# Feed-forward tiles finished in the attention slots: tanh and two products from PSUM, and one stored tile instead of two

## The chip, the cores and the metric

The kernel runs on one core of a Trainium2 chip. The metric is the device time of one execution in microseconds, as the median of several runs; smaller is better. TensorE (PE in the profile, PEld its weight loads) multiplies, VectorE (DVE), ScalarE (ACT) and GpSimd (POOL) work on elements, and SyncE (SP) issues most DMAs. Each engine takes its instructions in the order in which the program lists them, and engines wait for each other by semaphores.

## The reference

The layer mixes sliding-window attention and a gated feed-forward block by a sigmoid gate per row. S = 2048 rows, D = 512, 32 heads of 16, a window of 256, F = 1792.

```python
def _A_ref(x, wqkv, wo):                       # attention
    qkv = (x @ wqkv).reshape(B, S, 3, H, Dh) ...
    scores = einsum("bhqd,bhkd->bhqk", q, k) * (Dh ** -0.5)
    mask = (idx[:, None] - idx[None, :] >= 0) & (idx[:, None] - idx[None, :] < W)
    p = softmax(where(mask, scores, -1e9))
    return einsum("bhqk,bhkd->bhqd", p, v) ... @ wo
def _B_ref(x, w_gate, w_up, w_down):           # feed-forward
    return (silu(x @ w_gate) * (x @ w_up)) @ w_down
g = sigmoid((x * gate_w).sum(-1, keepdims=True))
return g * a + (1 - g) * b
```

## The kernel before

Every float32 product is made of three matmuls of a rounded high part and a low part (`xhi`, `xlo`, `wh`, `wl`), accumulated in PSUM. The work has three stages.

1. A start (about 80 us): x is split, q and k of the first two of eight head groups (four heads each) and all of v are computed, and the first scores of group 0.
2. The attention slots: 8 groups x 16 blocks = 128 slots t, with g = t // 16. A slot has four head steps. In each, `stage1` makes a score product of the next group for the row maximum (PE L275, tile `ps1`; DVE L277 masks it and takes the maximum, and so frees the PSUM bank), `stage2` makes a transposed score product of the present group (PE L314, tile `ps2`), whose exp ScalarE writes to `pt` (ACT L316) and GpSimd masks (L318, L321), and a "turn" adds six matmuls of 64 rows (PE L225), two at a time on the two halves of the array. In group 7 there is no `stage1` left, and `stage2` makes its score products two at a time. Every fourth slot (t % 4 = 0), after head step 1, `av` makes the weighted sum of 512 query rows (PE L338), which `finish` normalises in five steps over the following slots (L353 to L368).
3. The tail: the feed-forward's second product for all tiles and the output projection, 963 matmuls of 128 x 512.

The turns are projections that fill TensorE in the slots. A unit is one key: `("f", f, 0)` is the gate projection of feed-forward tile f (128 hidden columns by 2048 rows), `("f", f, 1)` its up projection, `("p", g)` the q and k of group g. `lanes` computes two 512-row chunks at once: in its first turn the first chunk gets the upper half of the contraction and the second chunk the lower half, in its second turn it is the other way round. The two turns write the same two banks from different halves of the array, so the second must not begin before the first is over. `lanes` sees to it by a dependence of the second turn's first matmuls on an instruction that follows the first turn:

```python
if second and i == 0:
    tc.add_manual_dep(mm.ins, BEHIND[mark[0]].ins.name, SYNC, reason="the first turn is over")
if i == n - 1:
    mark.append(len(BEHIND))
```

`BEHIND` is a list to which `stage2` appends each exp as it is written down (`stage1` appends its maxima in group 0 alone, ahead of the slots). `mark` holds the place of the next entry after the first turn's last matmul.

A unit takes four slots, with two pairs of chunks in banks `pa` and `pb` (each name has two banks): the order is `[a0, b0, a1, b1]`, one turn per slot. When a pair is done, ScalarE copies both banks to tiles `ev` (L522, `kept()`, five of them) and SP stores the copies in the DRAM array `raws` (L525). `AT` holds, for a slot and head step, the functions that `later` puts there; they run after that step's turn. The tail loads gate and up again (L689), ScalarE takes the silu (L703), VectorE multiplies (L704), and `split` makes the high and the low part for the second product. The tile of f = 13 alone is computed in the tail (L700). `prepare` splits the next unit's weights (ScalarE L67, GpSimd L70) and fetches the weights after those.

The order on each engine is the order in which this code is written out; no scheduler moves anything.

Of the kernel before, what the change touches and what calls it, by code (L numbers as in the profile page):

```python
# [9 lines left out]
F32 = mybir.dt.float32  # L10
# [23 lines left out]
def gated_mix(ctx, tc, xT, xn, wqk, wv, wo, wgu, wd, gw, out):  # L34
# [114 lines left out]

    WKEYS = list(UNITS)  # L150
    WKEYS += [("f", NF - 1, i) for i in range(2)]
# [22 lines left out]
    with ExitStack() as A:  # L174
# [151 lines left out]
        def av(g, c):  # L326


            AV[g, c] = (pp.tile([P, CH], F32, name="pb" if 4 * g + c + 1 < len(UNITS) else "pa"),
                        ps1.tile([P, CH], F32, name="ps1") if 4 * g + c + 1 >= 4 * (G - 1) else ps2.tile([P, CH], F32, name="ps2"))  # L330

            orders = [[4 * c + m for m in ms if 4 * c + m >= 0] for ms in ((0, 1, 2, -1, -2, 3), (0, 1, -1, 2, 3, -2))]
            for n, kbs in enumerate(zip(*orders)):
                for j in range(4):
                    for h, (o, kb) in enumerate(zip(HALVES, kbs)):
                        k0 = kb * P + 64 * h
                        q0, q1 = max(k0, c * CH), min(k0 + W + 64, c * CH + CH)
                        nc.tensor.matmul(AV[g, c][h][32 * j:32 * j + 32, q0 - c * CH:q1 - c * CH],  # L338
                                         VG[4 * g + kb // 4][o, kb % 4, 17 * j:17 * j + 32],
                                         PT[g, kb, j // 2][o, j % 2, q0 - kb * P:q1 - kb * P],  # L340
                                         start=n == 0, stop=n == len(orders[0]) - 1, skip_group_check=True)
# [170 lines left out]
        def unit(key, t):  # L512


            later(t, 3, prepare)

            def done(hf):
                def copies(ps):
                    t0 = t + 3 + hf
                    places = [kept(), kept()]  # L520
                    for m in range(2):
                        later(t0, 2 * m if t0 < G * NB else 0, lambda m=m: nc.scalar.copy(places[m], ps[m]))  # L522
                    if key[0] == "f":
                        for m in range(2):
                            later(t0 + 1, 2, lambda m=m: nc.sync.dma_start(raws[key[1], key[2], 2 * hf + m], places[m]))  # L525
                        return
                    g = key[1]

                    def half(m):
                        if m == 0:  # L530
                            X[g, hf] = x_pair()
                        split_qk(g, hf, m, places[m])
                    t1 = t0 + 3 * hf
                    later(t1, 3, lambda: half(0))
                    later(t1 + 1, 1, lambda: half(1))
                    later(t1 + 1, 3, lambda: stack(g, hf))
                return copies
# [43 lines left out]
        def tile0_load():  # L581
            for i, place in enumerate(halves_of(halves_of(KT[1][1])[0])):
                GOT[ORDER[0], i, 0] = place.bitcast(F32)
                nc.sync.dma_start(GOT[ORDER[0], i, 0], raws[ORDER[0], i, 0])

        def tile0():
            (gt, up), sg = [GOT.pop((ORDER[0], i, 0)) for i in range(2)], kept()
            nc.scalar.activation(sg, gt, AF.Silu)
            nc.vector.tensor_tensor(out=sg, in0=up, in1=sg, op=ALU.mult)
            split(*TILE0, sg, nc.scalar, nc.vector)  # L590
# [7 lines left out]
        for t in range(G * NB + 1):  # L598
            g, i = divmod(t, NB)
            d, part = divmod(t, NSLOT)  # L600
            if part == 0:
                turns = unit(UNITS[d], t) if d < len(UNITS) else [iter(())] * NSLOT
            s1 = stage1(g + 1, i) if t < g7 else iter(())
            s2 = stage2(g, i) if t < G * NB else iter(())
            for hd in range(4):
# [5 lines left out]
                run(turns[part], 3)  # L611
# [20 lines left out]
    with ExitStack() as B:  # L632
        hp = B.enter_context(tc.tile_pool(name="hp", bufs=3, side="right"))
        got = B.enter_context(tc.tile_pool(name="got", bufs=4, side="right"))
# [50 lines left out]
        def load_kept(c, f):  # L685

            for i in range(2):
                GOT[f, i, c] = got.tile([P, CH], F32, name=f"got{i}")
                nc.sync.dma_start(GOT[f, i, c], raws[f, i, c])  # L689

        def hidden(c, f):
            gu = []
            for i, name in enumerate(("pa", "pb")):
                if (f, i, c) in KEPT:
                    gu.append(GOT.pop((f, i, c)))
                    continue
# [6 lines left out]
            nc.scalar.activation(sg, gu[0], AF.Silu)  # L703
            nc.vector.tensor_tensor(out=sg, in0=gu[1], in1=sg, op=ALU.mult)  # L704
# [46 lines left out]
        for _ in range(3):  # L751
            load_kept(*loads.pop(0))
# [64 lines left out]
```

## Time and profile before

| | |
|---|---|
| median of 3 runs | 822.22 us (821.8 to 822.39) |
| span of the profiled execution, first to last instruction | 821.5 us |
| slots / tail in it | about 79.5 to 599 / 599 to 821.5 us |
| busy share of PE, DVE, ACT, POOL | 99%, 63%, 55%, 43% |
| granted TensorE clock | 1.000 |
| instructions | 21573 |

The page of the profile gives no other time of the profiled execution than its span. Rows of a timeline have the start and the length in us, engine, source line, operation, output tile <- input tiles, shape, and in brackets the idle time ahead of it and what ended it. A group's row has count, busy us and mean ns of one, and idle time ahead with its releasers. Matmul lengths are modelled, and neighbours overlap; what counts is the distance of their starts.

### The profile page before, as it was taken

How to read it: one execution, taken by the hardware profiler on the slowest of the kernel's cores; microseconds unless marked ns; L12 is line 12 of the kernel's file. 1: busy time of each engine (PE TensorE's matmuls, PEld its weight loads, DVE VectorE, ACT ScalarE, POOL GpSimd, SP SyncE). 2: the span in 40 equal slices, each digit the busy share in tenths (PEclk: the TensorE clock that was granted, in tenths of full speed). 3: DMA queues.
4: the chain of work that ended last, by engine and by line, in shares of the span. 5: the costliest groups of instructions: out<-in, count | busy, mean ns of one | idle time of the engine just before them, and what ended most of it. 6: DMA issues, size and time to landing. Idle time of an engine off the chain costs nothing.

```text
span 821.5 us, 21573 instructions
## 1 busy us (share of the span) xinstructions
PE 815.1 (99%) x8329; PEld 683.8 (83%) x8329; DVE 515.6 (63%) x1437; ACT 448.9 (55%) x936; POOL 351.8 (43%) x640
## 2 busy tenths in 40 slices
PE   8999999999999999999999999999999999999998
PEld 7888988888888888888888888888887888888886
DVE  6397677677667676677677667756567453443543
ACT  6422666666656666666666666656654433333341
POOL 7812555555546555645554655456511221011020
PEclk9999999999999999999999999999999999999999
DMA  8574534624534543552562463466698563383531
GB/s 294 164 206 150 154 121 125 191 94 146 166 128 125 161 146 117 152 170 101 144 193 102 126 191 125 160 207 201 210 325 267 182 197 110 131 244 107 178 125 51
DMA packets 67957, 133.26 MB, mean 162 GB/s; under 512 B 11600, under 2 KB 16336, under 8 KB 67856
## 3 DMA queue, kind: packets, MB, share of 16 engines
q1 hardware_dynamic: 63888, 118.00, 46.3%
q0 software_dynamic: 3968, 13.90, 4.6%
q8 instruction: 65, 1.06, 0.6%
q14 instruction: 36, 0.29, 0.1%
HBM read 61.08 MB, written 45.61 MB: 130 GB/s over the span
## 4 chain that ended last, share of the span: by engine, by line
PE 95%; DMA 2%; DVE 1%; ACT 1%; issue 1%; SPq 0%; DVEq 0%; ACTq 0%
PE pb L225 24%; PE pa L225 24%; PE pb L338 7%; PE ps L275 6%; PE ps L87 5%; PE ps L85 5%; PE ps L86 5%; PE ps L314 5%; PE pb L205 2%; PE pa L205 2%; PE pb L85 2%; PE pb L87 2%; PE pb L86 2%; PE ps L338 2%; DMA got<-raws 1%; PE pb L700 1%
## 5 line engine op out<-in xcount | busy, mean ns | idle before, releaser
L277 DVE CUSTOM_DVE_ANT_0 ps<-ps,mask 128x384 f32<-128x384 f32 (+2 forms) x512 | 271.6, 539 | 143.2 <-PE ps L314 66.7
L316 ACT ACTIVATE pt<-ps 128x384 f32<-128x384 f32 (+2 forms) x512 | 240.7, 477 | 114.9 <-PE ps L275 57.7
L318 POOL TENSOR_SCALAR_AFFINE_SELECT pt<-pt 128x256 f32<-128x256 f32 x256 | 107.4, 419 | 223.8 <-ACT pt L316 220.4
L314 PE MATMUL ps<-q,k 64*128 64x384 f32 (+2 forms) x512 | 159.9, 329 | 0.0
L275 PE MATMUL ps<-k,q 63*128 63x384 f32 (+2 forms) x512 | 158.7, 330 | 0.0
L225 PE MATMUL pb<-xhi,wh 64*128 64x512 f32 x512 | 111.3, 394 | 0.0
L225 PE MATMUL pb<-xlo,wh 64*128 64x512 f32 x512 | 110.1, 391 | 0.0
L225 PE MATMUL pb<-xhi,wl 64*128 64x512 f32 x512 | 109.9, 392 | 0.0
L225 PE MATMUL pa<-xhi,wh 64*128 64x512 f32 x512 | 109.0, 394 | 0.0
L225 PE MATMUL pa<-xhi,wl 64*128 64x512 f32 x512 | 107.9, 391 | 0.0
L225 PE MATMUL pa<-xlo,wh 64*128 64x512 f32 x512 | 107.8, 391 | 0.0
L275 PEld LDWEIGHTS ps<-k,q 63*128 63x128 f32 x512 | 88.8, 185 | 16.9 <-issue 5.7
L321 POOL TENSOR_SCALAR_AFFINE_SELECT pt<-pt 128x256 f32<-128x256 f32 x224 | 98.7, 441 | 0.0
L314 PEld LDWEIGHTS ps<-q,k 64*128 64x128 f32 x512 | 89.9, 184 | 5.4 <-issue 0.8
L704 DVE TENSOR_TENSOR sg<-got,sg 128x512 f32<-128x512 f32 x51 | 45.1, 885 | 64.6 <-ACT sg L703 59.9
L338 PE MATMUL ps<-pt,vg 64*32 64x320 f32 (+4 forms) x1408 | 75.0, 346 | 0.0
L338 PE MATMUL pb<-pt,vg 64*32 64x320 f32 (+3 forms) x1360 | 73.9, 350 | 0.0
L277 DVE DVE_READ_ACCUMULATOR2_ANT mx<- 128x1 f32 x512 | 71.9, 140 | 0.0
L338 PEld LDWEIGHTS pb<-pt,vg 64*32 64x32 f32 x1360 | 46.4, 106 | 28.3 <-ACT pt L316 9.9
L225 PEld LDWEIGHTS pb<-xhi,wh 64*128 64x128 f32 x512 | 56.6, 185 | 7.9 <-ACT ev L522 0.3
L225 PEld LDWEIGHTS pb<-xhi,wl 64*128 64x128 f32 x512 | 56.5, 184 | 6.7
L225 PEld LDWEIGHTS pa<-xhi,wl 64*128 64x128 f32 x512 | 54.7, 184 | 7.4
(159 smaller groups left out, 1576.6 us busy)
## 6 DMA issues: line engine op xcount, KB each, us to landing
raws<-ev SPq DMA_DIRECT2D x104, 256.0 KB
got<-raws SPq DMA_DIRECT2D x102, 256.0 KB
od<-o POOLq DMA_DIRECT2D x32, 256.0 KB, 2.6
raw<-wgu SPq DMA_DIRECT2D x28, 256.0 KB
q<-xhi SPq DMA_DIRECT2D x56, 128.0 KB
k<-xhi SPq DMA_DIRECT2D x56, 128.0 KB
vd<-vs POOLq DMA_DIRECT2D x8, 672.0 KB, 5.1
vg<-vd SPq DMA_DIRECT2D x32, 168.0 KB
```

Of the source, the lines that this page charges most:

```text
L85: nc.tensor.matmul(ps, lh, rh, start=start and i == 0, stop=False, skip_group_check=skip)
L86: nc.tensor.matmul(ps, lh, rl, start=False, stop=False, skip_group_check=skip)
L87: nc.tensor.matmul(ps, ll, rh, start=False, stop=stop and i == n - 1, skip_group_check=skip)
L225: mm = nc.tensor.matmul(ps[me], w[r], x[r], start=not second and i == 0, stop=bool(second) and i == n - 1)
L275: nc.tensor.matmul(ps[:, :n], QT[g % 2][pr][r, q0:q0 + P], KT[g % 2][pr][r, k0:k0 + n], start=True, stop=True)
L277: mx = nc.vector.tensor_tensor_reduce(out=ps[:, :n], in0=ps[:, :n], in1=mask[:, 3 * P - n:], scale=1.0, scalar=NEG, op0=ALU.add, op1=ALU.m ...
L314: nc.tensor.matmul(ps[:, :n], KT[g % 2][pr][r, k0:k0 + P], QT[g % 2][pr][r, k0:k0 + n], start=True, stop=True)
L316: BEHIND.append(nc.scalar.activation(pt[:, j, :n], ps[:, :n], AF.Exp, scale=SCALE))
L318: nc.gpsimd.affine_select(out=pt[:, :, :P], in_=pt[:, :, :P], pattern=[[0, 2], [1, P]], compare_op=ALU.is_ge, fill=0.0, base=0, channel_mu ...
L321: nc.gpsimd.affine_select(out=pt[:, :, 2 * P:], in_=pt[:, :, 2 * P:], pattern=[[0, 2], [-1, P]], compare_op=ALU.is_ge, fill=0.0, base=-1, ...
L338: nc.tensor.matmul(AV[g, c][h][32 * j:32 * j + 32, q0 - c * CH:q1 - c * CH], VG[4 * g + kb // 4][o, kb % 4, 17 * j:17 * j + 32], PT[g, kb, ...
L704: nc.vector.tensor_tensor(out=sg, in0=gu[1], in1=sg, op=ALU.mult)
```

## The change

A feed-forward tile is finished in the slots. The turns now come as halves, each with its own kind of end: a gate half, an up half or a group half, two slots each (`TURNS`, 64 of them). For a gate half ScalarE writes t = tanh(g / 2) to an `ev` tile (L526) and VectorE forms (t + 1) * g in place (L529); for the up half that follows VectorE forms that * 0.5 * u (L541), which is silu(g) * u. Both VectorE products read PSUM and free its banks. One tile per chunk is stored in `kept_h` (L544) and loaded in the tail (`load_kept`), where silu and product fall away; 52 + 51 transfers of 256 KB take the place of 104 + 102, and six loads are issued ahead instead of three. The tile of f = 13 uses the same tanh and products in the tail. `prepare` stands two slots ahead of a key's first turn. `lanes` is not changed, nor are `stage1`, `stage2` and `av`. In the changed kernel L225 is L229, L275 L279, L277 L281, L314 L318, L316 L320, L338 L342 and L522 (for group halves) L554.

```diff
-    early = [("f", f, i) for f in range(NF - 1) for i in range(2)]
-    KEPT = {(f, i, c) for _, f, i in early for c in range(NCH)}
-    UNITS = []
+    KEPT = {(f, c) for f in range(NF - 1) for c in range(NCH)}
+    tiles = iter([[(("f", f, i), hf) for i in range(2)] for f in range(NF - 1) for hf in range(2)])
+    TURNS = []
     for g in range(2, G):
-        UNITS += early[:2] + [("p", g)] + early[2:3]
-        early = early[3:]
-    UNITS += early
-    raws = dram.tile([NF - 1, 2, NCH, P, CH], F32, name="raws")
+        for n in range(4):
+            TURNS += [(("p", g), hf) for hf in range(2)] if n == 2 - g % 2 else next(tiles)
+    for two in tiles:
+        TURNS += two
...
+    kept_h = dram.tile([NF - 1, NCH, P, CH], F32, name="kept_h")
...
-                    t0 = t + 3 + hf
-                    places = [kept(), kept()]
-                    for m in range(2):
-                        later(t0, 2 * m if t0 < G * NB else 0, lambda m=m: nc.scalar.copy(places[m], ps[m]))
-                    if key[0] == "f":
-                        for m in range(2):
-                            later(t0 + 1, 2, lambda m=m: nc.sync.dma_start(raws[key[1], key[2], 2 * hf + m], places[m]))
...
-            (a0, a1), (b0, b1) = (lanes(pp, name, [products(key, 2 * hf + m) for m in range(2)], done(hf))
-                                  for hf, name in enumerate(("pa", "pb")))
-            return [a0, b0, a1, b1]
+        for key in KEYS[1:-1]:
+            later(FIRST[key] - 2, 1, prepare)
...
+        def gate_half(t, f, hf):
...
+                def tanh(m):
+                    SIL[f, hf, m] = kept()
+                    nc.scalar.activation(SIL[f, hf, m], ps[m], AF.Tanh, scale=0.5)
...
+                    nc.vector.scalar_tensor_tensor(SIL[f, hf, m], SIL[f, hf, m], 1.0, ps[m], op0=ALU.add, op1=ALU.mult)
+                for m in range(2):
+                    later(t + 2 + m, 0, lambda m=m: tanh(m))
+                    later(t + 2 + m, 3 - m, lambda m=m: product(m))
...
+        def up_half(t, f, hf):
...
+                    nc.vector.scalar_tensor_tensor(hs[m], hs[m], 0.5, ps[m], op0=ALU.mult, op1=ALU.mult)
+                for m in range(2):
+                    later(t + 2, 3 * m if t + 2 < G * NB else 0, lambda m=m: product(m))
+                    later(t + 3, 2, lambda m=m: nc.sync.dma_start(kept_h[f, 2 * hf + m], hs[m]))
...
+        def unit(n):
+
+            t, (key, hf) = 2 * n, TURNS[n]
+            done = group_half(t, key[1], hf) if key[0] == "p" else (gate_half, up_half)[key[2]](t, key[1], hf)
+            return lanes(pp, ("pa", "pb")[n % 2], [products(key, 2 * hf + m) for m in range(2)], done)
...
-            if part == 0:
-                turns = unit(UNITS[d], t) if d < len(UNITS) else [iter(())] * NSLOT
+            if t % 2 == 0:
+                turns = unit(t // 2) if t < G * NB else [iter(())] * 2
...
-                run(turns[part], 3)
+                run(turns[t % 2], 3)
...
-                if (f, i, c) in KEPT:
-                    gu.append(GOT.pop((f, i, c)))
-                    continue
...
+            if (f, c) in KEPT:
+                return GOT.pop((f, c))
```

What moves is shown on two engines. The names behind "waits" are semaphores; one of an engine's name counts that engine's instructions. First TensorE, before, in slot 10, where the second turn of the pair in `pa` begins (L225 with `pa`), behind a turn of the pair in `pb`:

```order
L225 MATMUL pb_1694<-xhi2_75,wl_1377 128x512
L225 MATMUL pb_1695<-xhi3_77,wl_1377 128x512
L275 MATMUL ps1_1746<-k10_360,q10_358 128x384 [waits DVE_49]
L314 MATMUL ps2_1750<-q00_90,k00_92 128x384 [waits Activation_49]
L225 MATMUL pa_1577<-xhi1_73,wh_1376 128x512
L225 MATMUL pa_1576<-xhi0_71,wh_1376 128x512
```

TensorE in the changed kernel, from the end of the first turn of a pair in `pa` (slot 8) over the beginning of its second turn (slot 9):

```order
L229 MATMUL pa_1574<-xhi0_71,wl_1463 128x512
L229 MATMUL pa_1575<-xhi1_73,wl_1463 128x512
L279 MATMUL ps1_1677<-k10_360,q10_358 128x384 [waits DVE_49]
L318 MATMUL ps2_1681<-q00_90,k00_92 128x384 [waits Activation_49]
L229 MATMUL pa_1575<-xhi1_73,wh_1462 128x512 [waits Activation_49]
L229 MATMUL pa_1574<-xhi0_71,wh_1462 128x512
L229 MATMUL pa_1575<-xlo1_74,wh_1462 128x512
L229 MATMUL pa_1574<-xlo0_72,wh_1462 128x512
L229 MATMUL pa_1575<-xhi1_73,wl_1463 128x512
L229 MATMUL pa_1574<-xhi0_71,wl_1463 128x512
L279 MATMUL ps1_1690<-k10_360,q10_358 128x384 [waits DVE_49]
L318 MATMUL ps2_1693<-q00_90,k00_92 128x384
```

The second turn stood two slots behind the first and named no ScalarE instruction; now it stands in the next slot, its first matmul waits for ScalarE, and the score product of the next head step no longer does.

VectorE, before, around the border of slots 51 and 52 (t % 4 = 3 and 0), from the last step of `finish` on (L277 is a maximum, printed as two instructions):

```order
L367 STREAM_TRANSPOSE o1_1342<-o0_1341 128x512
L277 ISA ps1_4916,mx_4633<-ps1_4916,mask_119 128x384 [waits PE_49]
L277 ISA mx_4633 128x1
L277 ISA ps1_4930,mx_4633<-ps1_4930,mask_119 128x384 [waits PE_49]
L277 ISA mx_4633 128x1
L277 ISA ps1_4946,mx_4633<-ps1_4946,mask_119 128x384 [waits PE_49]
L277 ISA mx_4633 128x1
```

VectorE in the changed kernel at the same place:

```order
L371 STREAM_TRANSPOSE o1_1342<-o0_1341 128x512
L281 ISA ps1_4900,mx_4617<-ps1_4900,mask_119 128x384 [waits PE_49]
L281 ISA mx_4617 128x1
L529 SCALAR_TENSOR_TENSOR ev_4882<-ev_4882,pa_4626 128x512 [waits DMAHW4_49,Activation_49]
L281 ISA ps1_4914,mx_4617<-ps1_4914,mask_119 128x384 [waits PE_49]
L281 ISA mx_4617 128x1
L281 ISA ps1_4928,mx_4617<-ps1_4928,mask_119 128x384 [waits PE_49]
L281 ISA mx_4617 128x1
L541 SCALAR_TENSOR_TENSOR ev_4814<-ev_4814,pb_4806 128x512
L281 ISA ps1_4944,mx_4617<-ps1_4944,mask_119 128x384 [waits PE_49]
```

A gate product stands behind the maximum of head step 2 and an up product behind that of head step 0; both read a bank (`pa`, `pb`) that ScalarE's copy emptied before.

More of the change, by code (lines that the diff above doesn't have):

```diff
@@ new lines, in group_half, with done, half @@
+        def group_half(t, g, hf):
+            t0 = t + 2 + (not hf)
+            def done(ps):
+                places = [kept(), kept()]
+                for m in range(2):
+                    later(t0, 2 * m, lambda m=m: nc.scalar.copy(places[m], ps[m]))
+                def half(m):
+                    if m == 0:
+                        X[g, hf] = x_pair()
+                    split_qk(g, hf, m, places[m])
+                first = t0 + 3 * hf
+                later(first, 3, lambda: half(0))
+                later(first + 1, 1, lambda: half(1))
+                later(max(first + 1, (g - 1) * NB) if hf else first + 1, 3, lambda: stack(g, hf))
+            return done
@@ L633, in gated_mix @@
         hp = B.enter_context(tc.tile_pool(name="hp", bufs=3, side="right"))
[L634 removed]
+        got = B.enter_context(tc.tile_pool(name="got", bufs=8, side="right"))
         bp = B.enter_context(tc.tile_pool(name="bp", bufs=2))
@@ L750, in gated_mix @@
         loads = [(c, ORDER[n]) for c, n in seq if n != 1 and c + n]
-        for _ in range(3):
+        for _ in range(6):
             load_kept(*loads.pop(0))
```

52 lines of the change are left out of this document (22 added, 30 removed).

## The prediction

> **What bounds the kernel now.** I read the busy table and the chain first, then the windows by stage, and then the timeline of TensorE, ScalarE and VectorE inside single slots.
>
> ```profile
> PE 815.1 (99%) x8329; PEld 683.8 (83%) x8329; DVE 515.6 (63%) x1437; ACT 448.9 (55%) x936; POOL 351.8 (43%) x640
> ...
> PE 95%; DMA 2%; DVE 1%; ACT 1%; issue 1%; SPq 0%; DVEq 0%; ACTq 0%
> ...
> 0.00:50.00 50.00, 47.83 (x280) 39.04 (x282) 27.61 (x64) 25.67 (x45) 34.18 (x44) 1.00 0.73 221
> ...
> 139.00:531.00 392.00, 392.00 (x5186) 329.15 (x5184) 278.41 (x923) 250.85 (x551) 212.55 (x430) 1.00 0.46 144
> 531.00:599.00 68.00, 67.95 (x935) 58.27 (x932) 38.36 (x83) 42.83 (x100) 39.19 (x73) 1.00 0.62 211
> 599.00:821.50 222.50, 218.33 (x963) 180.16 (x963) 105.91 (x146) 85.46 (x150) 27.71 (x22) 1.00 0.54 172
> ```
>
> The window rows give PE, PEld, DVE, ACT, POOL, the granted clock, DMA share and GB/s. TensorE is busy in 392.00 of 392 us of attention, in 67.95 of 68 of the last head group and in 218.33 of 222.5 of the tail. So nothing that the change takes from ScalarE, from VectorE in the tail or from the DMAs is on the path. It pays only where TensorE itself waits now, and it costs wherever TensorE gets a new wait. Inside a slot TensorE runs to a strict beat:
>
> ```profile
> 318.68 0.33 PE L314 MATMUL ps<-q,k 64*128 64x384 f32 x1
> 318.85 0.39 PE L225 MATMUL pb<-xhi,wh 64*128 64x512 f32 x2
> ...
> 319.07 0.49 ACT L316 ACTIVATE pt<-ps 128x384 f32<-128x384 f32 x1 [0.37 <-PE ps L314]
> ...
> 319.04 0.57 DVE L277 CUSTOM_DVE_ANT_0 ps<-ps,mask 128x384 f32<-128x384 f32 x1 [0.22 <-PE ps L314]
> ...
> 302.06 0.33 PE L314 MATMUL ps<-q,k 64*128 64x384 f32 x1
> 302.23 0.40 PE L225 MATMUL pb<-xhi,wh 64*128 64x512 f32 x2
> ...
> 302.53 0.49 ACT L316 ACTIVATE pt<-ps 128x384 f32<-128x384 f32 x1 [0.44 <-PE ps L275]
> ```
>
> These are two slots with t % 4 = 3, at head step 0. The feed-forward matmul L225 follows the score product L314 by 0.17 us. The exp of that score product ends at 319.56 and 303.02, which is 0.71 and 0.79 us after L225 has started. Today nothing in L225 needs that exp.
>
> **The new wait.** `lanes` orders its second turn behind its first by a dependence on `BEHIND[mark[0]]`, the next instruction entered in that list after the first turn's last step. In the slots only `stage2` enters any: its exps. Before, the turns stand a0, b0, a1, b1, so a1 comes a whole slot after the exp that it must follow, and the wait is long met. Now a unit is a0, a1 in slots t and t+1. The entry after a0 is the exp of head step 0 of slot t+1, and a1's first matmul is written directly behind that exp's own score product. The order of the changed kernel shows it: that matmul waits for ScalarE, and the next L318, which used to name ScalarE, no longer does, since an exp that young has been waited for. TensorE is in order, so all that stands behind a1 waits too, and no other engine can cover it, because TensorE is the bound.
>
> There are 64 turns in the 128 slots (26 gate, 26 up, 12 group halves), so 64 such waits. Their price is the time from the normal start of L225 to the end of the exp, plus the restart. The restart shows where TensorE waited before:
>
> ```profile
> 7.95 1.87 ACT L67 CAST xhi<-q 128x512 fp32r<-128x512 f32 x3 [1.10 <-DMA q<-xT]
> ...
> 8.62 0.19 PEld L205 LDWEIGHTS pa<-xhi,wh 128*128 128x128 f32 x1 [0.80 <-ACT xhi L67]
> ...
> 8.62 0.50 PE L205 MATMUL pa<-xhi,wh 128*128 128x512 f32 x1 [0.49 <-ACT xhi L67]
> 8.95 0.39 PE L205 MATMUL pa<-xhi,wl 128*128 128x512 f32 x1
> ...
> 625.53 1.78 DVE L70 TENSOR_TENSOR hl<-sg,hh 128x512 fp32r<-128x512 f32 x1
> ...
> 626.63 0.39 PE L86 MATMUL ps<-q,hh 128*128 128x512 f32 x1
> 627.37 0.50 PE L87 MATMUL ps<-q,hl 128*128 128x512 f32 x1 [0.36 <-DVE hl L70]
> 627.71 0.40 PE L85 MATMUL ps<-q,hh 128*128 128x512 f32 x1
> ```
>
> VectorE's subtraction ends at 627.31 and TensorE starts at 627.37: 0.06 us. Its next matmul comes 0.34 us later where 0.23 is the beat: 0.11 more. The restart is 0.17 us. [...]
>
> Narrow blocks and the last head group (no stage 1, two score products at a time, the wait being for the first one's exp) have rows of their own:
>
> ```profile
> 335.20 0.51 PE L225 MATMUL pb<-xhi,wh 64*128 64x512 f32 x2
> ...
> 335.55 0.28 ACT L316 ACTIVATE pt<-ps 128x128 f32<-128x128 f32 x1 [0.48 <-PE ps L275]
> ...
> 562.30 0.47 PE L225 MATMUL pb<-xhi,wh 64*128 64x512 f32 x2
> ...
> 562.64 0.87 ACT L316 ACTIVATE pt<-ps 128x384 f32<-128x384 f32 x2 [0.69 <-PE ps L314]
> ```
>
> The last block of a group ends its exp at 335.83, 0.63 after L225. In the last group the first exp ends about 0.49 after 562.64, at 563.13, 0.83 after L225. Of the 64 waits, 8 are in the last block of their group, 7 more in the last group. So: 49 waits x (0.75 + 0.17) = 45.1; 8 narrow ones x (0.63 + 0.17) = 6.4; 7 in the last group x (0.83 + 0.17) = 7.0. Sum 58.5 us. Without the restart, and with 0.71 for the 49, it is 34.8 + 5.0 + 5.8 = 45.6.
>
> **The products on VectorE.** 52 (t+1)*g and 52 *u products, 128x512 from PSUM, come into the slots. None stands there now; the nearest rows are other products from PSUM:
>
> ```profile
> L355 DVE TENSOR_TENSOR o<-pb,o 128x512 f32<-128x512 f32 (+1 forms) x31 | 20.8, 671 | 11.5 <-ACT o L353 11.1 <-ACT pt L316 0.2
> L704 DVE TENSOR_TENSOR sg<-got,sg 128x512 f32<-128x512 f32 x51 | 45.1, 885 | 64.6 <-ACT sg L703 59.9 <-DMA got<-raws 4.7
> L675 DVE SCALAR_TENSOR_TENSOR k<-ps,igate,k 128x512 f32<-128x512 f32 x8 | 5.4, 742 | 0.0
> ...
> 287.31 0.57 DVE L277 CUSTOM_DVE_ANT_0 ps<-ps,mask 128x384 f32<-128x384 f32 x1 [0.26 <-PE ps L275]
> ...
> 287.79 0.71 DVE L367 STREAM_TRANSPOSE o<-o 128x512 f32<-128x512 f32 x1
> 288.42 0.54 DVE L277 CUSTOM_DVE_ANT_0 ps<-ps,mask 128x384 f32<-128x384 f32 x1
> ```
>
> I take L675's 0.742, the same operation on a PSUM operand; the ends are 0.671 and 0.885. VectorE has 278.41 of 392 us busy; 104 x 0.742 = 77 us over the whole slots still fit. But a product frees a PSUM bank that a ScalarE copy freed before, so its lateness counts. Two places are tight. A head step is 0.87 us (the three L225 pairs at 0.23 and the score products at 0.17). Count from the start of head step 1 of a slot t % 4 = 3, with the max L277 starting 0.36 us after its score product (319.04 against 318.68), 0.48 us from a max and 0.63 from a transpose to the next instruction, and, with the same overlap of 0.08, 0.66 from a product. Then the queue holds: max 0.36, transpose 0.84, max 1.47, gate product 1.95 to 2.69, max 2.61, max 3.09, up product 3.57 to 4.31; TensorE sees the ends 0.06 later, at 2.75 and 4.37. The next gate's first matmul wants its bank at 3 x 0.87 + 0.17 = 2.78. The weighted sum L342 wants the up product's bank after head step 1 of the next slot, at some 5 x 0.87 + 0.10 = 4.45 (the 0.10 by the rows of the second rival). Neither waits at 0.742. At 0.885 the ends come at 2.90 and, one product later, 4.66; the two wait 0.12 and 0.21, with the restart of 0.11 for the matmuls behind 0.23 and 0.32; that is 26 x 0.23 + 25 x 0.32 = 14.0 us. I take 1 us, near the low end, and keep both.
>
> **What is taken away.** 104 copies leave the slots and 52 tanhs come; ScalarE was not the bound. 51 silus and 51 products of 885 ns leave the tail, where TensorE hardly waited. The one stall there, the 0.51 us at 627.37 above the 0.23 beat, lies behind a VectorE subtraction of 1.78 us in a crowded queue; with fewer products there I let it go: -0.5 (0 at the other end). One table load goes:
>
> ```profile
> L588 ACT ACT_TABLE_LOAD x1 | 1.3, 1283 | 0.0
> ...
> raws<-ev SPq DMA_DIRECT2D x104, 256.0 KB
> got<-raws SPq DMA_DIRECT2D x102, 256.0 KB
> ```
>
> That load is beside L700's matmuls and is worth nothing. Half of the 206 transfers go, at a DMA share of 0.46 to 0.62: nothing. A `kept_h` store stands in SP's queue over a slot behind its product, as the old ones did behind their copies, so what is queued behind it doesn't wait more. Weight preparation moves to a head step two slots ahead of use: a 0.63 us cast and a 1.28 us subtraction within 7 us, nothing.
>
> **Sum.** 58.5 + 1 - 0.5 = 59.0 on the span of 821.5, so 880.5. The median of the runs is 0.7 above that span: 881.2 us.
>
> **Rivals.**
> - VectorE late as well: the products cost 0.885, as L704 did on SBUF operands. Time 881.2 + 13.0 = 894.2. Against it: L355 and L675, with a PSUM operand, are shorter, and each stall of the new kind gives VectorE 0.9 us to catch up.
> - No wait, and a little faster. If the exp named were the one a head earlier, it would end 0.88 - 0.87 = 0.01 us after its successor's score product starts, within L225's 0.17 us, and it would cost nothing; that is the point at which it decides. Then the gains stand alone: the 0.5 in the tail, and the start of the weighted sum, which now comes 0.33 us after the last L225 instead of 0.23, and 31 times behind ScalarE:
>
> ```profile
> PEld pb L338 <- ACT pt L316: 9.9, 27, 0.4
> ...
> PEld pb L338 <- ACT ev L522: 1.6, 4, 0.5
> ...
> 307.05 0.40 PE L225 MATMUL pa<-xhi,wl 64*128 64x512 f32 x2
> 307.38 0.45 PE L338 MATMUL pb<-pt,vg 64*32 64x320 f32 x1
> ```
>
>  31 x 0.10 + 0.5 = 3.6 less, 818.6. Against it stands the order: the next score product's own ScalarE wait is gone, so the newest exp is meant.
> - The clock falls. A tenth of the 460 us of the two attention windows at half the clock would add 46 us, 927 in all. The granted clock was 1.00 in the first 50 us, where TensorE idled for 2.2 us in all; the new gaps are 0.9 us long and some 8 us apart. [...]
>
> **How the numbers follow.** The waits with VectorE about on time: 0.84, 866 to 893, where 881.2 less 10.9 of restarts, 1.7 of the shorter sample and 3.1 of earlier weighted sums is 866, and the products' other 13.0 us would end at 894. VectorE late beyond 893: 0.07. Waits cheaper than all bounds, 830 to 866: 0.04. No wait: 0.03. The clock: 0.02. The first alone fills the range. About 0.2% (1.6 us) is what a measurement tells from no change: faster 0.02, same 0.01, slower 0.97.
>
> **What the profile of after would show.** Right: in the waits a row of TensorE's loads or matmuls of L229 released by ACT pt L320, some 64 times and 45 to 60 us; the 65.3 us of a head group, two of whose rows are
>
> ```profile
> 205.56 0.76 PE pb L225 x6
> ...
> 270.90 0.76 PE pb L225 x6
> ```
>
> stretched by 8 x 0.92 to some 72.7; a tail of still about 222 us; one table load; products L529 and L541 near 0.74. Wrong: L229's row absent, with groups of 65 us; L342 or L229 released by DVE L541 or L529 for more than 10 us; a granted clock under 1.00 in the slots.

## The result and the profile after

The changed kernel takes 891.63 us (median of 4 runs, 891.42 to 892.99); the kernel before took 822.31 us beside it. The ratio is 1.0848, with a 95% interval of [1.0832, 1.0863]: 69.3 us slower. Forecast were 881.2 us and a range of 866 to 893. The span of the profiled execution is 889.9 us, 68.4 more than before's.

The busy table, the chain by engine and the windows of the changed kernel (same columns as before's; the windows lie at the same places of the program):

```profile
PE 835.4 (94%) x8329; PEld 680.1 (76%) x8329; DVE 531.6 (60%) x1493; ACT 401.0 (45%) x831; POOL 347.5 (39%) x640
...
PE 89%; DVE 4%; ACT 4%; issue 1%; DMA 1%; POOL 0%; SPq 0%; ACTq 0%; DVEq 0%; POOLq 0%
...
150.00:590.00 440.00, 404.92 (x5161) 328.50 (x5160) 314.55 (x991) 237.08 (x509) 211.33 (x427) 1.00 0.34 105
590.00:662.00 72.00, 63.48 (x795) 48.27 (x791) 40.83 (x91) 33.71 (x79) 33.32 (x67) 0.98 0.42 140
667.00:889.90 222.90, 219.05 (x1027) 181.36 (x1011) 75.48 (x102) 56.17 (x96) 27.26 (x22) 1.00 0.35 114
```

ScalarE and the DMAs did get lighter (ScalarE 448.9 to 401.0 us, DMA share 0.46 to 0.34), and nothing came of it. TensorE, which was busy in every one of 392 us of attention, now idles for 35 of 440, and for 8.5 of 72 in the last group. The tail is where it was. On the chain stand ScalarE and VectorE with 4% each, about 36 us each. Who makes TensorE wait is in the waits (waiting engine, tile, line, releaser: us in all, times, longest):

```profile
PEld pa L229 <- ACT pt L320: 32.0, 32, 1.1
PEld pb L229 <- ACT pt L320: 30.4, 32, 1.1
...
PE pa L229 <- ACT pt L320: 20.7, 32, 0.7
PE pb L229 <- ACT pt L320: 18.6, 32, 0.7
...
PEld pb L342 <- DVE ev L541: 17.2, 23, 3.0
...
PE pb L342 <- DVE ev L541: 8.0, 9, 2.6
```

There are the 64 waits on the exp, and a second kind that the forecast held for nearly free: the weighted sum's bank, which waits for the second up product. One wait of the first kind, in the timeline:

```profile
321.60 0.33 PE L318 MATMUL ps<-q,k 64*128 64x384 f32 x1
322.01 0.49 ACT L320 ACTIVATE pt<-ps 128x384 f32<-128x384 f32 x1 [0.39 <-PE ps L279]
322.56 0.19 PEld L229 LDWEIGHTS pa<-xhi,wh 64*128 64x128 f32 x2 [0.99 <-ACT pt L320]
322.56 0.50 PE L229 MATMUL pa<-xhi,wh 64*128 64x512 f32 x2 [0.61 <-ACT pt L320]
322.67 0.19 PEld L229 LDWEIGHTS pa<-xlo,wh 64*128 64x128 f32 x2
322.90 0.40 PE L229 MATMUL pa<-xlo,wh 64*128 64x512 f32 x2
```

Without a wait L229 would start 0.17 us behind its score product, at 321.77. The exp ends at 322.50, TensorE starts at 322.56, and its next pair comes after 0.34 instead of 0.23: 0.73 + 0.06 + 0.11 = 0.90 us. The weight load stands in the same wait and starts together with the matmul.

I compared the starts of all 512 score products (L314 and L318) in both traces, head step by head step, to see where the 68.4 us lie. The start is 0.7 shorter. In groups 0 to 6 the 49 waits on a full exp cost 0.954 each and the 7 narrow ones 0.707: 51.7 us. The last group's 8 are 6.5 in all. The head steps with the weighted sum lost 6.1 in groups 0 to 6, and in the last group 1.2 in slot 112 and 5.3 in slot 120. What follows the last score product is 0.9 shorter, all other head steps together 0.8. That makes 68.4. (E4 and E1 speak against the 0.7 and the 0.9 as gains of the change; see below.) A head group takes (591.93 - 149.33) / 6 = 73.8 us instead of 65.4; 72.7 was forecast.

**The second kind of wait** has two sources. One is at the start of groups 1, 3 and 5, counted from 0 (E8's expectation counts them from 1):

```profile
149.86 1.29 POOL L70 TENSOR_TENSOR xlo<-ev,xhi 128x512 fp32r<-128x512 f32 x1 [0.24 <-ACT xhi L67]
149.96 1.23 DVE L292 TENSOR_SCALAR mt<-mx 128x32 fp32r<-128x32 f32 x1
151.54 0.68 DVE L541 SCALAR_TENSOR_TENSOR ev<-ev,pb 128x512 f32<-128x512 f32 x1
152.28 0.45 PE L342 MATMUL pb<-pt,vg 64*32 64x320 f32 x1 [1.06 <-DVE ev L541]
```

VectorE's small negation of the maxima (`put_max`, 0.18 us at its shortest, 0.28 in the median) takes 1.23 us and ends with GpSimd's subtraction; the up product behind it in the queue frees the bank 1.06 us too late. Seven more weighted sums that come right behind a `put_max` lost 0.22 to 0.52 us each; at four of them (slots 8, 40, 72, 104) the negation took 0.38 us and ended with GpSimd's mask L325. A loss of 0.85 us at slot 110, where VectorE's L368 took 1.47 us beside GpSimd's L70 and the maxima behind it came late, is among the other head steps. The other source is the last group:

```profile
626.73 0.72 DVE L585 SCALAR_TENSOR_TENSOR xhi<-xlo,xhi 128x512 f32<-128x512 f32 x1 [4.20 <-DMA xlo<-xn]
628.12 0.50 PE L229 MATMUL pa<-xhi,wh 64*128 64x512 f32 x1 [0.93 <-DVE ev L529]
629.56 0.79 DVE L69 CAST q<-ev 128x512 fp32r<-128x512 f32 x1 [1.50 <-DMA ev<-wd]
631.60 0.68 DVE L541 SCALAR_TENSOR_TENSOR ev<-ev,pb 128x512 f32<-128x512 f32 x1
632.34 0.74 PE L342 MATMUL pb<-pt,vg 64*32 64x320 f32 x1 [2.57 <-DVE ev L541]
...
629.70:631.98 2.28, 0.07 (x1) 0.00 (x0) 2.25 (x5) 0.00 (x0) 0.36 (x1) 1.00 0.39 90
631.98:635.39 3.41, 3.05 (x56) 1.43 (x64) 0.30 (x1) 0.00 (x0) 0.00 (x0) 0.50 0.62 208
635.39:638.80 3.41, 2.93 (x72) 2.19 (x56) 1.76 (x3) 1.75 (x5) 0.77 (x2) 1.00 0.32 121
```

VectorE's weighted sum for the gate (L585) waits 4.20 us for its rows of x, the early cast of the down weights (L69) another 1.50 us, both DMAs, and the products stand behind them in VectorE's queue. Before, VectorE waited for the same DMAs (8.3 us ahead of the gate's sums in this group) and TensorE was busy all the same, in 67.95 of 68 us: ScalarE's copies freed the banks then. TensorE is empty for 2.57 us, and then the granted clock is 0.50 for 3.41 us.

### The profile page after: what moved, and what is told of

Read it like the earlier page. It is cut to its first block, busy times and chain, and to the rows that moved or that the text cites. A ratio compares the mean times of both kernels' runs of the same rounds, so it can differ in the third digit from the quotient of the medians.

```text
span 889.9 us, 21379 instructions
## 1 busy us (share of the span) xinstructions
PE 835.4 (94%) x8329; PEld 680.1 (76%) x8329; DVE 531.6 (60%) x1493; ACT 401.0 (45%) x831; POOL 347.5 (39%) x640
## 3 DMA queue, kind: packets, MB, share of 16 engines
q8 instruction: 65, 1.06, 0.5%
## 4 chain that ended last, share of the span: by engine, by line
PE 89%; DVE 4%; ACT 4%; issue 1%; DMA 1%; POOL 0%; SPq 0%; ACTq 0%; DVEq 0%; POOLq 0%
PE pa L229 22%; PE pb L229 20%; PE pb L342 7%; PE ps L87 6%; PE ps L86 6%; PE ps L85 6%; PE ps L279 5%; PE ps L318 4%; ACT pt L320 4%; PE pa L209 2%; PE pb L209 2%; DVE ps L281 2%; PE ps L342 2%; PE pb L87 2%; PE pb L86 2%; PE pb L85 2%
## 5 line engine op out<-in xcount | busy, mean ns | idle before, releaser
L281 DVE CUSTOM_DVE_ANT_0 ps<-ps,mask 128x384 f32<-128x384 f32 (+2 forms) x512 | 270.5, 538 | 157.6 <-PE ps L279 85.6
L320 ACT ACTIVATE pt<-ps 128x384 f32<-128x384 f32 (+2 forms) x512 | 238.8, 473 | 192.4 <-PE ps L279 117.6
L322 POOL TENSOR_SCALAR_AFFINE_SELECT pt<-pt 128x256 f32<-128x256 f32 x256 | 107.3, 419 | 295.9 <-ACT pt L320 295.1
L279 PE MATMUL ps<-k,q 63*128 63x384 f32 (+2 forms) x512 | 158.9, 330 | 0.7 <-DVE mx L281 0.7
L318 PE MATMUL ps<-q,k 64*128 64x384 f32 (+2 forms) x512 | 159.0, 331 | 0.0
L229 PE MATMUL pa<-xhi,wh 64*128 64x512 f32 x512 | 111.5, 408 | 21.9 <-ACT pt L320 20.7
L229 PE MATMUL pb<-xhi,wh 64*128 64x512 f32 x512 | 110.1, 406 | 18.6 <-ACT pt L320 18.6
L229 PE MATMUL pa<-xlo,wh 64*128 64x512 f32 x512 | 106.9, 392 | 0.0
L229 PE MATMUL pa<-xhi,wl 64*128 64x512 f32 x512 | 106.6, 391 | 0.0
L229 PE MATMUL pb<-xlo,wh 64*128 64x512 f32 x512 | 106.0, 391 | 0.0
L229 PE MATMUL pb<-xhi,wl 64*128 64x512 f32 x512 | 106.0, 391 | 0.0
L70 DVE TENSOR_TENSOR hl<-got,hh 128x512 fp32r<-128x512 f32 x51 | 44.8, 882 | 95.7 <-ACT hh L67 95.7
L279 PEld LDWEIGHTS ps<-k,q 63*128 63x128 f32 x512 | 89.0, 185 | 14.6 <-issue 5.5
L318 PEld LDWEIGHTS ps<-q,k 64*128 64x128 f32 x512 | 89.7, 185 | 8.6 <-issue 0.8
L325 POOL TENSOR_SCALAR_AFFINE_SELECT pt<-pt 128x256 f32<-128x256 f32 x224 | 95.8, 428 | 0.0
L229 PEld LDWEIGHTS pa<-xhi,wh 64*128 64x128 f32 x512 | 53.6, 185 | 40.1 <-ACT pt L320 32.0
L342 PE MATMUL pb<-pt,vg 64*32 64x320 f32 (+3 forms) x1360 | 75.4, 356 | 8.0 <-DVE ev L541 8.0
L229 PEld LDWEIGHTS pb<-xhi,wh 64*128 64x128 f32 x512 | 52.6, 185 | 36.5 <-ACT pt L320 30.4
L342 PE MATMUL ps<-pt,vg 64*32 64x320 f32 (+4 forms) x1408 | 76.5, 351 | 0.0
L342 PEld LDWEIGHTS pb<-pt,vg 64*32 64x32 f32 x1360 | 47.1, 108 | 37.7 <-DVE ev L541 17.2
L281 DVE DVE_READ_ACCUMULATOR2_ANT mx<- 128x1 f32 x512 | 71.6, 140 | 0.0
L229 PEld LDWEIGHTS pa<-xhi,wl 64*128 64x128 f32 x512 | 53.3, 185 | 8.4
```

The source lines that it names most:

```text
L70: lo_eng.tensor_tensor(out=lo, in0=src, in1=hi.bitcast(F32), op=ALU.subtract)
L229: mm = nc.tensor.matmul(ps[me], w[r], x[r], start=not second and i == 0, stop=bool(second) and i == n - 1)
L279: nc.tensor.matmul(ps[:, :n], QT[g % 2][pr][r, q0:q0 + P], KT[g % 2][pr][r, k0:k0 + n], start=True, stop=True)
L281: mx = nc.vector.tensor_tensor_reduce(out=ps[:, :n], in0=ps[:, :n], in1=mask[:, 3 * P - n:], scale=1.0, scalar=NEG, op0=ALU.add, op1=ALU.m ...
L318: nc.tensor.matmul(ps[:, :n], KT[g % 2][pr][r, k0:k0 + P], QT[g % 2][pr][r, k0:k0 + n], start=True, stop=True)
L320: BEHIND.append(nc.scalar.activation(pt[:, j, :n], ps[:, :n], AF.Exp, scale=SCALE))
```

## The experiments

The theory is that the order a0, a1, b0, b1 makes every unit wait for an exp of its own slot, for about 58 us, and that the rest is VectorE work ahead of the products in its queue. The main rival is that the finishing by products from PSUM is the cost. Each median is of 4 runs (E5 9, E9 11), ratios are to the kernel before on the same chip (822.0 to 822.4 us); "less" is against the changed kernel's 891.63 us, unless another run is named.

**E1, the order alone.** The kernel before, with

```diff
-            return [a0, b0, a1, b1]
+            return [a0, a1, b0, b1]
```

> The kernel before, with one edit: a pair of units runs its four turns as a0, a1, b0, b1 instead of a0, b0, a1, b1. Tiles are finished as before (ScalarE's copies and sigmoid, two tiles stored and loaded). Theory (the wait of a unit's second turn on the exp is the cost): 64 waits near 0.9 us, 50 to 60 us more than before, 872 to 882 us. Rival A (the cost comes from the products from PSUM on VectorE and from banks freed late): no change, 820 to 826 us. If both matter, the time lies between them and the missing part is A's.

Measured: 882.04 us, 1.0731 [1.0715, 1.0747], 60.0 us more. In its waits:

```profile
PEld pa L225 <- ACT pt L316: 36.0, 32, 1.2
PEld pb L225 <- ACT pt L316: 30.3, 32, 1.1
```

The same 64 waits, with every tile finished as before. By head steps the waits of groups 0 to 6 cost 53.4 us; the last group with the tail took 6.05 more. The order alone is 87% of the loss. That it lies 0.8 us from what was forecast for the whole change is chance: a full stall costs 0.990 us here, against 0.954 in the changed kernel and 0.92 in the forecast. Why it is dearer here, no run shows.

**E2, the order undone, the finishing kept.** The changed kernel, with the turns of two units interleaved again:

```diff
-            t, (key, hf) = 2 * n, TURNS[n]
+            t, (key, hf) = n // 2 * 4 + 1 + n % 2, TURNS[n]
...
-            if t % 2 == 0:
-                turns = unit(t // 2) if t < G * NB else [iter(())] * 2
+            if part == 0:
+                turns = [iter(())] * 4
+            if part < 2 and t < G * NB:
+                turns[part], turns[part + 2] = unit(2 * d + part)
...
-                    later(t + 2 + m, 0, lambda m=m: tanh(m))
-                    later(t + 2 + m, 3 - m, lambda m=m: product(m))
+                    later(t + 2, m, lambda m=m: tanh(m))
+                    later(t + 2, m + 1, lambda m=m: product(m))
...
-                    later(t + 2, 3 * m if t + 2 < G * NB else 0, lambda m=m: product(m))
+                    later(t + 2, m if t + 2 < G * NB else 0, lambda m=m: product(m))
```

`FIRST`, `prepare`, the group halves' copies and one step of `finish` follow the new places.

> The changed kernel with the turns of two units interleaved again (a0, b0, a1, b1), so that a unit's second turn comes two slots after its first and the exp it asks for has long ended; tanh, the products and the one stored tile stay, the products one head step after their tanh. Theory (exp wait): the 64 waits go, 55 to 60 us less than the changed kernel, 830 to 838 us; what VectorE's late products still cost stays in it. Rival A (products from PSUM are the cost): 880 us or more, since they all stand. Rival B (banks are now held too long, because four are in use at a time and VectorE frees them): 845 to 870 us, with the first matmuls of a turn waiting for L529 or L541 instead of for the exp.

Measured: 842.19 us, 1.0240 [1.0223, 1.0258], 49.4 us less than the changed kernel. L229 waits for no exp any more. It is 4 us outside the theory's range, towards rival B, and the waits say why:

```profile
PEld pb L342 <- DVE ev L541: 13.2, 24, 1.5
PEld pa L229 <- DVE ev L529: 8.8, 8, 3.3
...
559.71 2.26 DVE L585 SCALAR_TENSOR_TENSOR xhi<-xlo,xhi 128x512 f32<-128x512 f32 x1
563.26 0.67 DVE L529 SCALAR_TENSOR_TENSOR ev<-ev,pa 128x512 f32<-128x512 f32 x1
563.99 0.79 PE L229 MATMUL pa<-xhi,wh 64*128 64x512 f32 x1 [2.93 <-DVE ev L529]
```

VectorE's lateness is still there: 6.8 us at the weighted sum in groups 0 to 6, and 9.8 us in the last group and the tail.

**E3, up products earlier.** The changed kernel, with

```diff
-                    later(t + 2, 3 * m if t + 2 < G * NB else 0, lambda m=m: product(m))
+                    later(t + 1 + m, 3 * (1 - m), lambda m=m: product(m))
```

> The changed kernel with the two up products put at head steps (t+1, 3) and (t+2, 0) instead of (t+2, 0) and (t+2, 3); nothing else moves. Theory (the part of the loss that the forecast missed is the weighted sum's bank, which waits for the second up product some 6 us in all): the waits of L342 on L541 go and 5 to 8 us with them, 883 to 887 us. Rival C (that wait only stands where PE would have waited for the exp anyway): under 1.5 us, 890 to 892 us. The waits on the exp stay at 64.

Measured: 886.33 us, 1.0778 [1.0762, 1.0794], 5.3 less. The head step of the weighted sum lost 0.6 us in groups 0 to 6 instead of 6.1. What is left of the wait,

```profile
PEld pb L342 <- DVE ev L541: 5.0, 4, 3.0
```

is four waits, one of them that in the last group.

**E4, the gate's work behind the products.** The changed kernel, with

```diff
-            later(t + 1, 2 + b % 2, lambda b=b: gate_block(b))
+            later(t + 2, 1, lambda b=b: gate_block(b))
...
-            later(t, 2, lambda: later(t + 1, 2, load_wd(f, piece, kept())))
+            later(t, 2, lambda: later(*((t + 2, 1) if t + 2 < G * NB else (t + 1, 2)), load_wd(f, piece, kept())))
```

> The changed kernel with VectorE's two kinds of work in the last group that wait for a DMA (the gate's weighted sum L585 and the cast of the early down weights) put two or three head steps later, behind the products instead of ahead of them; the same loads at the same places. Theory (these instructions hold the products up in VectorE's queue, and the TensorE gap that follows sets off the 3.4 us at half clock at 632 us): 4 to 6 us less, 886 to 888 us, and no stretch at half clock before the tail. Rival D (the last group's extra is ScalarE's or the DMA queue's and not the products'): 890 to 892 us.

Measured: 887.27 us, 1.0789 [1.0773, 1.0805], 4.4 less. Last group and tail lost 4.3 us instead of 11.1, so the instructions that wait for DMAs were the cause there. But the expectation on the clock failed: 3.41 us at half clock stand at 590 us now. The edit put the two L585 of slot 109 one behind the other into slot 110, ahead of `finish` and of the maxima, where VectorE was full, and group 6 lost 2.2 us more by it. The same place is seen more clearly in the next run.

**E7, E3 and E4 together.**

> E3 and E4 together: up products earlier, the gate's and the early down weights' work later. Theory (they take away two different waits, and what is left over the kernel before is the 64 waits on the exp): 5.3 and 4.4 us add up, 891.6 - 9.7 = 882 us, which is E1's time. Rival (one wait, seen twice): 886 us.

Measured: 881.39 us, 1.0718 [1.0701, 1.0734], 10.2 less: the two add up (5.3 + 4.4). What is left is the waits on the exp and this:

```profile
580.15 0.77 DVE L585 SCALAR_TENSOR_TENSOR xhi<-xlo,xhi 128x512 f32<-128x512 f32 x1
...
581.12 1.20 DVE L368 TENSOR_TENSOR o<-o,rc 128x256 f32<-128x256 f32 x1
...
582.91 0.44 PE L279 MATMUL ps<-k,q 63*128 63x384 f32 x1 [1.64 <-DVE mx L281]
...
584.06:587.47 3.41, 3.41 (x20) 3.10 (x18) 2.05 (x6) 0.69 (x3) 0.87 (x2) 0.50 0.59 213
587.47:590.88 3.41, 3.41 (x44) 2.52 (x49) 3.32 (x10) 1.66 (x4) 1.41 (x5) 1.00 0.19 77
```

The maxima L281 are late behind two L585 and behind L368. That L368 took 1.20 us, where the median of its 32 is 0.49: GpSimd's subtraction L70 ran until 582.04 beside it.

**E10, E7 with the gate's work in the last group**, two slots later, where there are no maxima:

```diff
-        later(g7 - 4, 1, gate_place)
+        later(g7 - 2, 1, gate_place)
...
-            t = g7 - 4 + b // 2 * 2
+            t = g7 - 2 + b // 2 * 2
...
-        later(g7 + NB - 3, 0, gate_end)
+        later(g7 + NB - 1, 0, gate_end)
```

> E7 with the gate's fetches and weighted sums two slots later, as in E9; the order a0, a1, b0, b1 stays. In E7 a TensorE gap of 1.64 us at 581 us, where score products wait for VectorE's maxima behind two sums L585, is followed by 3.41 us at half clock. Theory: the gap and the half clock go together, 1.6 + 1.7 = 3.3 us less than E7, 878 us, with no stretch at half clock before the end; what is then left over the kernel before, 56 us, is the 64 waits on the exp less what the tail gains. Rival J (the half clock comes from the place in the program or from the load on the whole, not from the gap): it stays, and the time is 880 us.

Measured: 877.90 us, 1.0676 [1.0661, 1.0690], 3.5 less than E7, with no half clock before the end. At the same place:

```profile
582.00:592.00 10.00, 9.48 (x156) 7.58 (x156) 8.49 (x20) 4.37 (x12) 4.15 (x8) 1.00 0.52 169
```

Gap and half clock went together, as the theory had it. Both causes of the gap went at once, though: the two L585 are gone from there and L368 takes 0.48 us, so this run doesn't part them. 55.5 us over the kernel before are left: the 64 waits, less small gains.

**E8, GpSimd's subtraction moved.** The changed kernel, with

```diff
-                later(first, 3, lambda: half(0))
+                later(first + 1, 0, lambda: half(0))
```

> The changed kernel with the first split of a projection's tile one head step later, (first + 1, 0) instead of (first, 3), so that GpSimd's subtraction L70 no longer runs while VectorE negates the maxima (L292) at the start of groups 2, 4 and 6. Theory (VectorE's L292 takes 1.23 instead of 0.18 us because it stands still until GpSimd's subtraction is over, and the up product behind it is late by that much): L292 takes 0.18 us everywhere and 3 waits of 1.26 us become short, 3 to 4 us less, 888 us. Rival G (L292 is long for another reason, such as its operand or the group's start): it stays at 1.2 us, 891 to 892 us.

Measured: 889.50 us, 1.0819 [1.0804, 1.0833], 2.1 less. L292 gets short as the theory had it, the size was too high:

```profile
149.95 0.18 DVE L292 TENSOR_SCALAR mt<-mx 128x32 fp32r<-128x32 f32 x1
150.49 0.68 DVE L541 SCALAR_TENSOR_TENSOR ev<-ev,pb 128x512 f32<-128x512 f32 x1
150.75 1.28 POOL L70 TENSOR_TENSOR xlo<-ev,xhi 128x512 fp32r<-128x512 f32 x1 [1.14 <-ACT xhi L67]
```

L292 is back at 0.18 us (0.40 at most over all 16; 1.23 in the changed kernel), and the three losses of 1.26 us at the weighted sum became 0.19 to 0.26. Others of them grew by 0.1 to 0.2 each, so 2.3 of 6.1 us went there.

**E6, the exp cut in two.** The changed kernel, with

```diff
-                BEHIND.append(nc.scalar.activation(pt[:, j, :n], ps[:, :n], AF.Exp, scale=SCALE))
+                cut = P if kb % 2 and hd == 1 and n > P else n
+                BEHIND.append(nc.scalar.activation(pt[:, j, :cut], ps[:, :cut], AF.Exp, scale=SCALE))
+                if cut < n:
+                    nc.scalar.activation(pt[:, j, cut:n], ps[:, cut:n], AF.Exp, scale=SCALE)
```

> The changed kernel with the first exp of each odd slot cut in two, 128 columns first and 256 behind; the second turn waits for the first piece. In rows the exp of 384 columns takes 493 ns and that of 128 columns 277 ns. Theory (the price of a stall is the score product and then the exp up to its end, so it follows the exp's length): 56 of the 64 stalls become 0.216 us shorter, 12 us less, 878 to 881 us (the other 8 wait for an exp of 128 columns already). Rival F (the price is a fixed cost of stopping and restarting TensorE): 890 to 893 us, with the wait unchanged. ScalarE gets 56 instructions more, which is under 4 us in all and lies beside TensorE's work.

Measured: 880.05 us, 1.0705 [1.0691, 1.0720], 11.6 less, against 12.1 expected. The wait now ends with the first piece:

```profile
316.13 0.34 PE L318 MATMUL ps<-q,k 64*128 64x384 f32 x1
316.52 0.28 ACT L321 ACTIVATE pt<-ps 128x128 f32<-128x128 f32 x1 [0.37 <-PE ps L318]
316.70 0.38 ACT L323 ACTIVATE pt<-ps 128x256 f32<-128x256 f32 x1
316.85 0.50 PE L229 MATMUL pa<-xhi,wh 64*128 64x512 f32 x2 [0.39 <-ACT pt L321]
```

L229 starts 0.72 us behind its score product instead of 0.96. The price is the path from score product to the exp's end, not a fixed cost of stopping.

**E5, E2 with VectorE's late work moved.** To E2's edits come those of E3 and E4, and tanh and gate products one place earlier:

```diff
-                    later(t + 2, m, lambda m=m: tanh(m))
-                    later(t + 2, m + 1, lambda m=m: product(m))
+                    later(t + 1 + m, 3 * (1 - m), lambda m=m: tanh(m))
+                    later(t + 2, m, lambda m=m: product(m))
```

> E2 with VectorE's late work moved: the first of the two tanh and of the two up products right behind the unit's last matmul (t+1, 3) and the second at (t+2, 0), the gate's products at (t+2, 0) and (t+2, 1), and the gate's weighted sums and the early casts of the down weights two or three head steps later, as in E4. Theory (what E2 still lost is VectorE's lateness, 6.8 us at the weighted sum in groups 0 to 6 and 9.8 us in the last group): both go, 822 to 830 us, and if nothing else is late about the kernel before, 822 us. Rival E (the products from PSUM cost VectorE time that no order hides): 836 us or more. That it beats the kernel before by 0.5% would need a wait of before to go as well; I don't expect it.

Measured: 824.30 us, 1.0026 [1.0016, 1.0035]: 67 us less than the changed kernel, with all its tanhs, products and half its transfers.

**E9, E5 with its last two waits removed**: E10's edit, and the first `prepare` one head step earlier.

> E5 with its two remaining waits removed: the gate's fetches and weighted sums start two slots later, so that all of VectorE's sums L585 fall into the last group, which has no score maxima (E5 lost 1.26 us at 532 us there), and the first weights' split comes one head step earlier (E5 lost 0.8 us at 83 us). Theory: 824.3 - 2.1 = 822.2 us, the kernel before within what can be told apart. Rival H (the finishing by tanh and two products is itself dearer): 824 us again. Rival I (it is itself cheaper, since the tail's hidden tiles are loaded once: E5's last group and tail took 1.9 us less than before's): under 821 us.

Measured: 823.51 us, 1.0015 [1.0006, 1.0024]: 1.1 us above the kernel before, between the theory's 822.2 and rival H's 824. Without its stalls the changed kernel's finishing is not faster than what it replaced, but dearer by 0.5 to 2.0 us by the interval. Chain by engine and windows:

```profile
PE 99%; POOL 0%; ACT 0%; issue 0%; DVE 0%; DVEq 0%; POOLq 0%
...
150.00:535.00 385.00, 385.00 (x5040) 323.12 (x5038) 308.49 (x974) 234.69 (x503) 208.77 (x423) 1.00 0.39 118
535.00:600.00 65.00, 63.92 (x902) 53.27 (x900) 45.98 (x97) 36.08 (x85) 37.11 (x71) 1.00 0.51 169
600.00:821.30 221.30, 217.49 (x963) 180.06 (x961) 72.60 (x98) 56.30 (x96) 27.25 (x22) 1.00 0.36 114
```

TensorE is full again in attention. Relieving ScalarE and the DMAs buys nothing beside it. The last group holds one idle of TensorE, 1.08 us ahead of the last weighted sum:

```profile
594.58 1.29 POOL L70 TENSOR_TENSOR wl<-raw,wh 128x512 fp32r<-128x512 f32 x1
594.65 1.26 DVE L593 TENSOR_SCALAR gate<-gate 128x16 f32<-128x16 f32 x1 [2.07 <-ACT gate L592]
596.31 0.68 DVE L529 SCALAR_TENSOR_TENSOR ev<-ev,pa 128x512 f32<-128x512 f32 x1
597.10 0.43 PE L342 MATMUL pa<-pt,vg 64*32 64x320 f32 x1 [1.08 <-POOL pt L322]
```

The row names GpSimd's L322, but that had ended at 596.24; what ended right ahead of L342 is the gate product L529, at 596.99, which frees a bank `pa`. It stood behind L593, a small step of the gate, which took 1.26 us beside GpSimd's subtraction. The edit itself brought L593 to this place: in E5, two slots earlier, it took 0.43 us and the last weighted sum lost nothing. Without the idle, 823.5 - 1.1 = 822.4 us would be left, an estimate; no run takes it away, so rival H is not ruled out to the last microsecond.

## Why the prediction was right, and where it was short

- **The new wait: right, with its size.** 64 waits on ACT pt, 62.4 us by the loads' rows (45 to 60 were named, so a little more) and 51.7 + 6.5 = 58.2 us by the distances of head steps, against 58.5. A full stall measured 0.954 (0.92 assumed), a narrow one 0.707 (0.80), the last group's 0.81 on average (1.00). That these errors nearly cancel is luck. E1 shows that the order makes it, E2 and E5 that it goes with the order, E6 that its length is the exp's. That the second turn needs the first to be over is the program's own dependence; no run leaves it out.
- **The restart: right.** 0.06 + 0.11 us stand in the row at 322.56. The weight load starts together with its matmul there, behind the same wait.
- **The products on VectorE: the term that was mis-sized.** I took 1 us between 0 and 14. The duration was not at fault; the products were even shorter than assumed:

```profile
L529 DVE SCALAR_TENSOR_TENSOR ev<-ev,pa 128x512 f32<-128x512 f32 x52 | 35.5, 682 | 7.1 <-ACT ev L526 7.1
L541 DVE SCALAR_TENSOR_TENSOR ev<-ev,pb 128x512 f32<-128x512 f32 x52 | 35.4, 682 | 0.0
```

 What failed is the queue that I counted: one ordinary slot of maxima, a transpose and products, in which both places were met by 0.03 and 0.08 us. Slots with other VectorE work ahead (the negation that takes 1.23 us beside GpSimd's subtraction, the gate's sums, the casts that wait for DMAs) were not counted. Lateness cost 6.1 us in groups 0 to 6 (E3 took it away) and 1.2 + 5.3 in the last group (E4; about 1.7 of the 5.3 is the half clock), 12.6 against 1. That is 11.6 more; 0.3 less for the waits, 0.7 for the start, 0.4 for the tail and 0.8 for the rest leave the 9.4 by which the span was short of 889.9. Another 1.0 lies outside it: this median is 1.7 us above the profiled span, before's was 0.7. The 15 runs of the kernel before that were timed beside E9 all lie about 1.7 us above their own spans (820.1 to 821.9 us), so the profiled execution of before was about 1 us longer than its median run.
- **The range held in part by luck.** Its top, 1.4 us above the result, got 13.0 us from products of 0.885 us each. They took 0.682, and the lateness that the sum had not counted happened to cost about as much, 12.6. Two of the three signs of being wrong that the prediction names did stand in the profile: L342 and L229 released by L541 and L529 for 19.1 us by the loads' rows (9.1 by the matmuls'), and a granted clock of 0.98 in the last group. At the lower end, the 1.7 us for the shorter sample should be 49 x 0.04 = 2.0.
- **Taken away: nothing that is shown, the tail's 0.5 us included.** Start and tail are 0.7 and 0.9 us shorter than in before's trace. But E4, with the same start, took 0.3 us longer there than before, and E1, whose tail is finished as before, is shorter by the same 0.9: the stall at 627.37 stands in before's trace alone. So neither is shown to be a gain of the change; before's other executions were about 1 us shorter as a whole. One table load, half the transfers and ScalarE's copies gave nothing, as E9 shows for all of it together.
- **The rivals.** "VectorE late" named the right engine with the wrong mechanism: a slower product would have cost in every slot, and the losses stand at 12 of the 32 weighted sums. "The clock falls" came true once, for 3.41 us, about 1.7 us lost. The 64 stalls never set it off: E1 has them all, at up to 0.9 us of idle TensorE each, and no half clock ahead of its last 2 us; the granted clock over its whole span is 0.999.

## What to carry to other kernels

When an edit shortens the distance between an instruction and the event that it must follow, ask which event it is now and how old it will be; a dependence that was long met can become the youngest one there is, and its price is then the whole path to that event. When a bank or buffer is to be freed by another engine, read that engine's queue in every kind of slot, and above all for instructions ahead of the freeing one that wait for DMAs or that take longer beside another engine's work (here 1.23 us instead of 0.18). Work taken from engines that are not the bound is worth nothing until it is shown to end a wait of the one that is.

## What the runs showed of the hardware

- **The clock after one short gap.** 3.41 or 6.83 us at half clock followed TensorE gaps of 1.64 us (E4, E7), 2.23 (E6), 2.56 (E3, E8), 2.57 (the changed kernel) and 2.93 (E2, with a clock of 0.62 on average from 561 to 570 us). They began 2.2 us after the gap's start in the changed kernel and 2.8 us after it in E7. Gaps of 1.53 and 1.72 us in E2 were not followed by one, nor were the three of 1.05 and 1.06 us in the changed kernel (at 151, 298 and 446 us), the one of 1.1 us in E5 and the one of 1.08 us in E9 (1.00 in the windows around them). (Another gap, of 1.28 us in E6 and of 0.93 us in the changed kernel, ended 1.7 us ahead of the one of 2.23 and of 2.57.) A gap of 1.64 us was followed by half clock and one of 1.72 us was not; what decides it, no run shows.
- **A small VectorE operation beside GpSimd's subtraction.** L292, 32 elements per row, takes 0.18 us in E8 and 1.23 beside a GpSimd subtraction that began 0.10 us ahead of it; both end within 0.04 us of each other, and E8 parts them. Two other instructions of VectorE did the same beside L70: L368, 1.47 us in the changed kernel and 1.20 in E7 against at most 0.66 elsewhere in these two, and L593, 1.26 in E9 against 0.43 in E5 and in the changed kernel. The products, with an operand in PSUM, did not lengthen: in the changed kernel 19 of the 104 ran beside an L70 for 0.14 to 0.69 us and took 646 to 690 ns, the other 85 took 675 to 689 ns.
